# Loading w_in in whole rows, one channel chunk at a time, and holding back one block of x, in a convolution and two-layer MLP kernel

## Chip, cores, metric

One core of one Trainium2 chip. The metric is device microseconds (us) of an execution, lower is better. Most numbers below come from traces: an execution's span, counted from its first instruction, is about 1.7 us shorter than the time measured for it.

## The reference

```python
# x: (8, 4096, 192), weight: (8 heads, 7 taps), w_in: (192, 2048), w_out: (2048, 192)
w = softmax(weight, axis=-1)
y[b, s, h, g] = sum_k w[h, k] * x_pad[b, s + k, h, g]      # causal, 7 taps, 24 channels a head
h = y.reshape(32768, 192) @ w_in
out = maximum(0.01 * h, h) @ w_out                          # float32
```

## The kernel before

The listing is shortened; `...` marks the larger cuts. Two batch rows share the 128 partitions, 64 channels each; 192 channels are three chunks. So w_in is loaded twice, once for each half of the partitions, with a cast from float32 to bf16. The first two blocks of 512 positions go through the machine in halves of 256 ("half 0" to "half 3" of x). VectorE makes most of the convolution, TensorE the two matmuls, ScalarE evicts the first one with the leaky ReLU.

```python
    def load_first(q, after=None):            # x, half q, on the SyncE queue; two stage buffers
        t = stage_pool.tile([128, 2, HS, D], FP32, name="x_nat")
        ...                                   # "after": the load waits for that instruction

    w_in = const_pool.tile([128, NCH, F], BF16)
    for q in range(WQ):                       # WQ = 4 column quarters
        for e in range(2):                    # two halves of the partitions
            fs = slice(q * F // WQ, (q + 1) * F // WQ)
            nc.gpsimd.dma_start(
                out=w_in[e * CH : (e + 1) * CH, :, fs],
                in_=moe_w_in[:, fs].rearrange("(c p) f -> p c f", p=CH),
            )
    w_out = const_pool.tile([128, NFC, D], BF16)
    nc.gpsimd.dma_start(out=w_out, in_=moe_w_out.rearrange("(c p) d -> p c d", p=128))
    ...
    def mm1(grp, u):                          # one unit: 256 columns of h for 256 positions
        ph = psum_h.tile([128, 2, ST], FP32, name="ph", tag="ph")      # two buffers
        for i in range(nf):
            f = nf * u + i
            for c in range(NCH):              # all three chunks close one accumulation
                for e in range(2):
                    nc.tensor.matmul(out=ph[:, e, ...], lhsT=w_in[ps, c, f * 128 : (f + 1) * 128],
                                     rhs=y[ps, c, t0 : t0 + T], start=(c == 0), stop=(c == NCH - 1))
        act = nc.scalar.activation(out=g[blk][...], in_=ph..., func=Prelu, alpha=0.01)
    ...
    for i, grp in enumerate(groups):          # group 0 = half 0, group 1 = half 1, ...
        for j in range(steps):
            for u in range(2 * j, 2 * j + 2):
                mm1(grp, u)
                if i == 0 and u == 3:         # convolution of group 1, chunk 0, on TensorE
                    for job in pe_ahead:
                        job()
            ...                               # second matmul of the group before
            if i == 0 and j == 3:             # cast, transpose and copy half 2
                ...
                transpose_first(2)
                evac_first(2, nc.vector.tensor_copy, nc.vector.tensor_copy)
            for job in ahead[per * j : per * (j + 1)]:
                job()                         # VectorE: convolution of the next group
```

Of the kernel before, what the change touches and what calls it, by code (L numbers as in the profile page):

```python
# [14 lines left out]
def kernel(  # L15
# [8 lines left out]
    nc = tc.nc  # L24

    B, S, D = x.shape
    H, K = weight.shape
    Din, F = moe_w_in.shape
# [6 lines left out]
    CH = 64  # L35
    NCH = D // CH
# [5 lines left out]
    NB = S // ST  # L42
    NBLK = (B // 2) * NB
    LAG = NFC + NFC // 2
    WQ = 4
    NHALF = 5
    NPEC = 2

# [58 lines left out]
    def load_first(q, after=None):  # L107
        t = stage_pool.tile([128, 2, HS, D], FP32, name="x_nat")
        for e in range(2):
            ins = nc.sync.dma_start(  # L110
                out=t[:, e, :, :],
                in_=x[e, q * HT : (q + 1) * HT, :].rearrange("(c p) d -> p c d", p=128),
            )
            if after is not None and e == 0:
                tc.add_manual_dep(
                    ins.ins, after.ins.name,
                    mybir.DependencyInfo(
                        mybir.DependencyClass.Sync, mybir.DependencyReason.DATA
                    ),
                    reason="leave the DMA engines to w_in",  # L120
                )
        x_nat[q] = t

    def cast_first(q, e, copy):
        if q % 2 == 0 and e == 0:
            x_bf[q // 2] = xb_pool.tile([128, NCH, SUB, 2, CH], BF16, name="x_bf")
        h = q % 2
        copy(  # L128
            out=x_bf[q // 2][:, :, h * HS : (h + 1) * HS, e, :],
            in_=x_nat[q][:, e, :, :].rearrange("p s (c k) -> p c s k", c=NCH),  # L130
        )
# [20 lines left out]
    def evac_first(q, *copies):  # L152
        dst = xt[0][:, :, HALO + q * HT : HALO + (q + 1) * HT].rearrange(
            "p c (s i k) -> p i s c k", s=HS, i=2
        )
        for i, t in enumerate(ptr.pop(q)):
            copies[i](out=dst[:, i], in_=t)  # L157
# [4 lines left out]
    def conv_jobs(grp, chunks=range(NCH)):  # L162
        blk, t0, T = grp
        rp, st = divmod(blk, NB)
        if blk not in yt:
            yt[blk] = yt_pool.tile([128, NCH, ST], BF16, name="yt")
        y = yt[blk]
        jobs = []
        for c in chunks:
            for k in range(K):  # L170
                a = BASE + k + st * ST + t0
                src = xt[rp][:, c, a : a + T]
                dst = y[:, c, t0 : t0 + T]
                if k == 0:
                    jobs.append(
                        lambda s=src, d=dst, c=c: nc.vector.tensor_scalar_mul(  # L176
                            d, s, wk[:, c, 0:1]
                        )
                    )
                else:  # L180
                    jobs.append(
                        lambda s=src, d=dst, c=c, k=k: nc.vector.scalar_tensor_tensor(  # L182
                            out=d, in0=s, scalar=wk[:, c, k : k + 1], in1=d,
                            op0=mybir.AluOpType.mult, op1=mybir.AluOpType.add,
                        )
                    )
        return jobs
# [39 lines left out]
    for sign, off in ((1, 0), (-1, GRP - 1)):  # L227
        nc.gpsimd.affine_select(  # L228
            out=sel, in_=sel, compare_op=mybir.AluOpType.is_ge, fill=0.0,
            base=off, channel_multiplier=-sign * GRP,  # L230
            pattern=[[sign * CH, NCH], [0, 2], [sign, CH]],
        )

    w_in = const_pool.tile([128, NCH, F], BF16)
    for q in range(WQ):
        for e in range(2):
            fs = slice(q * F // WQ, (q + 1) * F // WQ)
            nc.gpsimd.dma_start(  # L238
                out=w_in[e * CH : (e + 1) * CH, :, fs],
                in_=moe_w_in[:, fs].rearrange("(c p) f -> p c f", p=CH),  # L240
            )
    w_out = const_pool.tile([128, NFC, D], BF16)
    nc.gpsimd.dma_start(out=w_out, in_=moe_w_out.rearrange("(c p) d -> p c d", p=128))
# [4 lines left out]
    def warm(n):  # L248
# [9 lines left out]
        out=nmax, in_=w9[:, 0:K], axis=mybir.AxisListType.X,  # L258
# [3 lines left out]
        out=w9[:, 0:K], in_=w9[:, 0:K], func=mybir.ActivationFunctionType.Exp,  # L262
# [33 lines left out]
    def diag_high(c):  # L296
        nc.vector.tensor_mul(
            diag[c][:, 0],
            ident2[:, None, :].to_broadcast([128, K, CH]),
            whm[:, c, 0, 0:K, None].to_broadcast([128, K, CH]),  # L300
        )

    def diag_low(c, ks):
        for k in ks:
            act = nc.scalar.activation(  # L305
                out=diag[c][:, 1, k, :], in_=ident2,
                func=mybir.ActivationFunctionType.Copy, scale=whm[:, c, 1, k : k + 1],
            )
        return act

    diag_high(0)
    cast_first(0, 0, nc.vector.tensor_copy)
# [10 lines left out]
    wk = const_pool.tile([128, NCH, K], FP32, name="wk")  # L323
    nc.vector.tensor_mul(wk, wraw[:, :, 0:K], rsum.to_broadcast([128, NCH, K]))
    evac_first(0, nc.vector.tensor_copy, nc.scalar.copy)
    low = diag_low(0, range(2, K))
    diag_high(1)
    diag_low(1, range(K))

# [2 lines left out]
            out=out, in_=in_, func=mybir.ActivationFunctionType.Copy, scale=scale  # L332
        )

    load_first(2, low)
    for n, job in enumerate(conv_jobs(groups[0], range(NPEC, NCH))):
        if n in (4, 5):
            cast_first(1, n - 4, nc.vector.tensor_copy)
        job()
    load_first(3)  # L340
    for c in range(NPEC):
        pe_jobs, evac_y = pe_conv_jobs(groups[0], c)
        for job in pe_jobs:
# [17 lines left out]
    def mm1(grp, u):  # L361
        blk, t0, T = grp
        y = yt[blk]
        nf = ST // T
        ph = psum_h.tile([128, 2, ST], FP32, name="ph", tag="ph")
        for i in range(nf):
            f = nf * u + i
            for c in range(NCH):
                for e in range(2):
                    ps = slice(e * CH, (e + 1) * CH)  # L370
                    nc.tensor.matmul(  # L371
                        out=ph[:, e, i * T : (i + 1) * T],
                        lhsT=w_in[ps, c, f * 128 : (f + 1) * 128],
                        rhs=y[ps, c, t0 : t0 + T],
                        start=(c == 0),
                        stop=(c == NCH - 1),
                    )
        act = nc.scalar.activation(  # L378
            out=g[blk][:, nf * u : nf * (u + 1), :, t0 : t0 + T],
            in_=ph.rearrange("p e (i t) -> p i e t", i=nf),  # L380
            func=mybir.ActivationFunctionType.Prelu, alpha=0.01,
        )
        while unsealed:
            seal[unsealed.pop()] = act.ins.name

    def mm2_one(rt, m, fc):
        b, e, s = subs[m]
# [23 lines left out]
    def mm2_slot(q):  # L411


        n, fc = divmod(q, NFC)
        if n < LAST:
            mm2_one(0, n, fc)
        t1 = q - LAG
        if t1 >= 0:
            mm2_one(1, *divmod(t1, NFC))
            if t1 % NFC == NFC - 1:  # L420
                evac_o(t1 // NFC)
# [18 lines left out]
    for i, grp in enumerate(groups):  # L440
        blk, t0, T = grp
        steps = T // 64
        if t0 == 0:
            g[blk] = g_pool.tile([128, NFC, 2, ST], BF16, name="g", tag="g")
        quota = (avail - slot) // steps

        if i == 0:
            ahead = []
        else:
            ahead = conv_jobs(groups[i + 1]) if i + 1 < len(groups) else []  # L450
        per = -(-len(ahead) // (steps - 1)) if T == ST else -(-len(ahead) // steps)
        for j in range(steps):
            for u in range(2 * j, 2 * j + 2):
                mm1(grp, u)
                if i == 0 and u == 0:
                    pe_ahead, evac_y = pe_conv_jobs(groups[1], 0)
                    ahead = conv_jobs(groups[1], range(1, NCH))
                    per = len(ahead)
                if i == 0 and u == 3:
                    for job in pe_ahead:  # L460
                        job()
                if i == 1 and u in (0, 2):
                    cast_first(3, u // 2, nc.scalar.copy)
            for _ in range(quota):
                mm2_slot(slot)
                slot += 1
            if i == 0 and j == 3:
                evac_y(nc.vector.tensor_scalar_mul)
                for e in range(2):
                    cast_first(2, e, nc.vector.tensor_copy)  # L470
                transpose_first(2)
                evac_first(2, nc.vector.tensor_copy, nc.vector.tensor_copy)
            if i == 1 and j == 1:

                nc.gpsimd.tensor_copy(out=pjunk, in_=g[0][0:1, NFC - 1, 1, HT - 1 : HT])  # L475
                load_x(2)
            if i == 2 and j == 1:
                transpose_x(2)
            for job in ahead[per * j : per * (j + 1)]:
                job()  # L480
            if i == 1 and j == 1:
                transpose_first(3)
                evac_first(3, nc.vector.tensor_copy, nc.vector.tensor_copy)

            last_half = t0 + T == ST
            if j == steps // 4 and last_half:
                load_x(blk + 3)
            if j == steps // 2 and last_half and blk > 0:
                transpose_x(blk + 2)
        avail += 2 * T // 128 * NFC  # L490
# [37 lines left out]
```

## Time and profile before

| | before |
|---|---|
| time, three runs | 698.39 us (698.24 to 699.26) |
| span of the trace | 698.3 us |
| TensorE busy | 689.0 us, 99% |
| first eviction starts | 12.03 us |
| w_in, last load lands | 18.98 us |
| w_out lands | 24.47 us |

TensorE is full from about 25 us to the end, so what a change of the first loads can move is when this full stretch begins. Lines that the prediction shows are not repeated. ScalarE's timeline (start, length, engine, instruction, idle time before it and what ended it):

```profile
12.03 1.94 ACT L378 ACTIVATE g<-ph 128x1024 bf16<-128x1024 f32 x2 [0.81 <-PE ph L371]
14.21 1.94 ACT L378 ACTIVATE g<-ph 128x1024 bf16<-128x1024 f32 x2 [0.24 <-PE ph L371]
17.31 1.94 ACT L378 ACTIVATE g<-ph 128x1024 bf16<-128x1024 f32 x2 [1.17 <-PE ph L371]
19.89 2.97 ACT L378 ACTIVATE g<-ph 128x1024 bf16<-128x1024 f32 x3 [0.64 <-PE ph L371]
```

Eight units of group 0 are evicted from 12.03 to 21.83 with idle gaps of about 2 us.

### The profile page before, as it was taken

What the parts mean: (1) busy time and instruction counts of PE and PEld (TensorE: products, weight loads), DVE (VectorE), ACT (ScalarE), POOL (GpSimd) and SP (SyncE); (2) the same over time, 40 slices, a digit from 0 to 9 for tenths busy, and PEclk for the clock granted to TensorE, in tenths of its full rate; (3) what the DMA queues carried; (4) which work ended last, traced back from release to release, by engine and by line L of the source; (5) the groups of instructions that cost most, each with busy time, mean ns of one, the idle gap of its engine ahead of it and who ended that gap; (6) DMA issues with size and microseconds to landing.
All of it is one profiled execution on the core that took longest, in us unless ns stands there. A gap on an engine that the chain in (4) does not pass through costs nothing.

```text
span 698.3 us, 26019 instructions
## 1 busy us (share of the span) xinstructions
PE 689.0 (99%) x11762; PEld 608.0 (87%) x11762; DVE 542.1 (78%) x1005; ACT 512.1 (73%) x576; POOL 142.3 (20%) x199
## 2 busy tenths in 40 slices
PE   8899999999999999999999999999999999999997
PEld 6799999678888888888888888888888888888887
DVE  7799999967777787777787777787777787777712
ACT  6688888977777777777777777777777777777770
POOL 4722220410222210222211222220222211000000
PEclk9999999999999999999999999999999999999999
DMA  9969554845555535555645556544566625122112
GB/s 170 115 83 104 83 71 81 86 71 76 77 74 83 89 67 76 77 74 84 86 67 79 69 81 81 88 73 71 77 75 81 92 63 77 54 52 58 47 36 69
DMA packets 184847, 54.39 MB, mean 78 GB/s; under 512 B 148384, under 2 KB 184736, under 8 KB 184736
## 3 DMA queue, kind: packets, MB, share of 16 engines
q0 software_dynamic: 98768, 14.17, 29.5%
q1 hardware_dynamic: 85968, 38.56, 23.2%
q8 instruction: 92, 1.51, 0.9%
q14 instruction: 19, 0.16, 0.1%
HBM read 29.88 MB, written 25.17 MB: 79 GB/s over the span
## 4 chain that ended last, share of the span: by engine, by line
PE 94%; DMA 3%; DVE 2%; POOL 0%; issue 0%; ACT 0%; POOLq 0%; ACTq 0%
PE po L391 48%; PE ph L371 46%; DMA w_out<-in_moe_w_out_dram 2%; DVE yt L182 2%; DMA w_in<-in_moe_w_in_dram 1%; POOL sel L228 0%; DVE yt L176 0%; ACT g L378 0%; POOL sel L226 0%; DVE o_sb L430 0%; POOL ident masks.py:199 0%; POOL ident masks.py:197 0%; PE ptr L143 0%; POOLq masks.py:199 0%; ACTq L430 0%
## 5 line engine op out<-in xcount | busy, mean ns | idle before, releaser
L378 ACT ACTIVATE g<-ph 128x1024 bf16<-128x1024 f32 x512 | 496.4, 1021 | 165.7 <-PE ph L371 165.7
L182 DVE SCALAR_TENSOR_TENSOR yt<-xt,wk,yt 128x512 bf16<-128x512 bf16 (+1 forms) x648 | 442.4, 683 | 17.6
L391 PE MATMUL po<-w_out,g 64*128 64x192 bf16 (+1 forms) x8048 | 398.4, 243 | 1.8 <-DMA w_out<-in_moe_w_out_dram 1.8
L391 PEld LDWEIGHTS <-g 64*128 64x128 bf16 (+1 forms) x8048 | 372.3, 94 | 31.1 <-issue 2.2
L371 PE MATMUL ph<-yt,w_in 64*128 64x512 bf16 (+1 forms) x3552 | 393.6, 348 | 2.2 <-ACT g L378 1.2
L371 PEld LDWEIGHTS <-w_in 64*128 64x128 bf16 x3552 | 247.8, 94 | 50.4 <-issue 3.9
L79 POOL DMA_DIRECT2D x_bf<-in_x_dram x180 | 133.7, 774 | 422.4 <-DMA xt<-x_bf 422.4
L430 DVE COPY o_sb<-po 128x192 f32<-128x192 f32 x216 | 77.2, 357 | 127.4 <-PE po L391 125.0
L176 DVE TENSOR_SCALAR yt<-xt,wk 128x512 bf16<-128x512 bf16 (+1 forms) x108 | 36.3, 336 | 0.1
L430 ACT COPY o_sb<-po 128x192 f32<-128x192 f32 x40 | 13.1, 327 | 0.0
L250 PE MATMUL warm<-zero 128*128 128x256 bf16 x24 | 5.2, 371 | 1.1 <-DVE junk L218 1.1
L157 DVE COPY xt<-ptr 128x384 bf16<-128x384 bf16 x7 | 2.2, 351 | 4.4 <-PE ptr L143 4.4
L201 PE MATMUL acc<-xt,diag 64*64 64x256 bf16 x84 | 5.2, 270 | 0.1
L238 POOL DMA_DIRECT2D w_in<-in_moe_w_in_dram x8 | 5.1, 643 | 0.0
L201 PEld LDWEIGHTS <-diag 64*64 64x64 bf16 x84 | 4.3, 106 | 0.8 <-DVE xt L157 0.4
L305 ACT ACTIVATE diag<-ident,whm 128x64 bf16<-128x64 bf16 x14 | 3.6, 335 | 1.9 <-DVE whm L291 1.9
L250 PEld LDWEIGHTS <-zero 128*128 128x128 bf16 x24 | 2.6, 125 | 2.1 <-DVE junk L218 1.1
L475 POOL COPY pjunk<-g 1x1 bf16<-1x1 bf16 x1 | 0.3, 312 | 10.9 <-ACT g L378 10.9
L143 PEld LDWEIGHTS <-x_bf 64*128 64x128 bf16 x48 | 1.4, 94 | 1.0 <-ACT x_bf L128 0.8
L143 PE MATMUL ptr<-ident,x_bf 64*128 64x64 bf16 x48 | 1.7, 191 | 0.5 <-DVE wraw L318 0.5
L128 DVE CAST x_bf<-x_nat 128x384 bf16<-128x384 f32 x5 | 2.2, 449 | 0.0
L255 ACT ACT_TABLE_LOAD x1 | 1.3, 1283 | 0.8 <-PEq L512 0.8
(34 smaller groups left out, 12.2 us busy)
## 6 DMA issues: line engine op xcount, KB each, us to landing
out_dram<-o_sb SPq DMA_DIRECT2D x128, 192.0 KB, 2.2
x_bf<-in_x_dram POOLq DMA_DIRECT2D x180, 64.0 KB, 3.1
x_nat<-in_x_dram SPq DMA_DIRECT2D x8, 192.0 KB, 5.6
w_in<-in_moe_w_in_dram POOLq DMA_DIRECT2D x8, 192.0 KB, 8.7
xt<-x_bf SPq DMA_TRANSPOSE x90, 2.4
w_out<-in_moe_w_out_dram POOLq DMA_DIRECT2D x1, 768.0 KB, 14.7
w<-in_weight_dram SPq DMA_DIRECT2D x1, 0.2 KB
```

The lines of the kernel that those rows point to most:

```text
L79: nc.gpsimd.dma_start(out=t[:, c, :, e, :], in_=src[2 * rp + e, :, :, c * CH : (c + 1) * CH],)
L143: nc.tensor.transpose(out=ts[i][:, s, c, :], in_=x_bf[q // 2][ps, c, (q % 2) * HS + s, :, :].rearrange("p e k -> p (e k)"), identity=ident ...
L176: lambda s=src, d=dst, c=c: nc.vector.tensor_scalar_mul(d, s, wk[:, c, 0:1])
L182: lambda s=src, d=dst, c=c, k=k: nc.vector.scalar_tensor_tensor(out=d, in0=s, scalar=wk[:, c, k : k + 1], in1=d, op0=mybir.AluOpType.mult, ...
L201: lambda k=k, p=p, a=a, e=e, ps=ps: nc.tensor.matmul(out=acc[ps, :T], lhsT=diag[c][ps, p, k, :], rhs=xt[0][ps, c, a : a + T], start=(k == ...
L238: nc.gpsimd.dma_start(out=w_in[e * CH : (e + 1) * CH, :, fs], in_=moe_w_in[:, fs].rearrange("(c p) f -> p c f", p=CH),)
L250: nc.tensor.matmul(out=wa[:, 0, 0:HT], lhsT=zero[:, 0:128], rhs=zero, start=True, stop=True)
L305: act = nc.scalar.activation(out=diag[c][:, 1, k, :], in_=ident2, func=mybir.ActivationFunctionType.Copy, scale=whm[:, c, 1, k : k + 1],)
L371: nc.tensor.matmul(out=ph[:, e, i * T : (i + 1) * T], lhsT=w_in[ps, c, f * 128 : (f + 1) * 128], rhs=y[ps, c, t0 : t0 + T], start=(c == 0) ...
L378: act = nc.scalar.activation(out=g[blk][:, nf * u : nf * (u + 1), :, t0 : t0 + T], in_=ph.rearrange("p e (i t) -> p i e t", i=nf), func=my ...
L391: ins = nc.tensor.matmul(out=po[m], lhsT=g[b][ps, fc, e, s * 128 : (s + 1) * 128], rhs=w_out[ps, fc, :], start=(rt != 1 and fc == 0), stop ...
L430: copy(out=o_sb[:, n % 2, :], in_=po.pop(n))
```

## The change

The intent: long contiguous rows instead of short pieces of columns, and fewer transfers beside the weights. w_in comes in six loads of whole rows (one chunk, one half of the partitions each). x's half 2 is no longer held until ScalarE has made the first diagonals; half 3 is held until the third eviction.

```diff
-    for q in range(WQ):
+    for c in range(NCH):
         for e in range(2):
-            fs = slice(q * F // WQ, (q + 1) * F // WQ)
             nc.gpsimd.dma_start(
-                out=w_in[e * CH : (e + 1) * CH, :, fs],
-                in_=moe_w_in[:, fs].rearrange("(c p) f -> p c f", p=CH),
+                out=w_in[e * CH : (e + 1) * CH, c, :], in_=moe_w_in[c * CH : (c + 1) * CH, :]
             )
...
-    load_first(2, low)
+    load_first(2)
...
-    load_first(3)
...
-                mm1(grp, u)
+                act = mm1(grp, u)
...
+                if i == 0 and u == 2:
+                    load_first(3, act)
```

More of the change, by code (lines that the diff above doesn't have):

```diff
@@ L44 @@
     LAG = NFC + NFC // 2
-    WQ = 4
     NHALF = 5
@@ L119, in load_first @@
                     ),
-                    reason="leave the DMA engines to w_in",
+                    reason="leave the DMA engines to the weights",
                 )
@@ L304, in diag_low @@
         for k in ks:
-            act = nc.scalar.activation(
+            nc.scalar.activation(
                 out=diag[c][:, 1, k, :], in_=ident2,
@@ L308, in diag_low @@
             )
-        return act
     diag_high(0)
@@ L325 @@
     evac_first(0, nc.vector.tensor_copy, nc.scalar.copy)
-    low = diag_low(0, range(2, K))
+    diag_low(0, range(2, K))
     diag_high(1)
@@ L384, in mm1 @@
             seal[unsealed.pop()] = act.ins.name
+        return act
     def mm2_one(rt, m, fc):
```

## The prediction

> **What bounds the kernel now.** I read the page first, then the chain of work that ended last, the waits, the transfers and clock of the first 30 us in windows, and the timelines of VectorE and TensorE up to 125 us. From the page:
>
> ```profile
> PE 689.0 (99%) x11762; PEld 608.0 (87%) x11762; DVE 542.1 (78%) x1005; ACT 512.1 (73%) x576; POOL 142.3 (20%) x199
> PE 94%; DMA 3%; DVE 2%; POOL 0%; issue 0%; ACT 0%; POOLq 0%; ACTq 0%
> ```
>
> TensorE is busy for 689.0 of 698.3 us. The change touches only the loads of the first 25 us, so all that it can move is the start; the 3% that the chain gives to DMA is this stretch of the chain:
>
> ```profile
> 2.90 6.58 DMA w_in<-in_moe_w_in_dram
> 9.48 0.28 issue
> 9.77 14.70 DMA w_out<-in_moe_w_out_dram
> 24.47 0.04 issue
> 24.51 1.33 PE po L391 x14
> ```
>
> The ninth GpSimd load (w_out, after eight of w_in) is issued only at 9.77, when the first w_in load has landed, and lands at 24.47; only then can the second matmul (po) start. The longest waits of the first 40 us that involve weights are small:
>
> ```profile
> PEld L371 <- DMA w_in<-in_moe_w_in_dram: 2.2, 2, 1.3
> PE po L391 <- DMA w_out<-in_moe_w_out_dram: 1.8, 1, 1.8
> POOL w_out L243 <- DMA w_in<-in_moe_w_in_dram: 1.8, 1, 1.8
> ```
>
> Windows on the clock show that the wait for w_out costs more than its 1.8 us (columns: stretch, then length and busy time of PE, PEld, DVE, ACT, POOL, then clock, DMA share, GB/s):
>
> ```profile
> 22.26:25.67 3.41, 1.61 (x25) 1.41 (x22) 3.23 (x7) 1.92 (x3) 3.41 (x5) 1.00 0.95 68
> 25.67:29.08 3.41, 3.41 (x32) 2.56 (x31) 1.48 (x4) 1.59 (x3) 3.41 (x6) 0.50 1.37 87
> ```
>
> After a window in which PE was busy for 1.61 us, it runs 3.41 us at half clock: 1.7 us lost.
>
> Last, a bound that the shares hide. VectorE's and TensorE's timelines:
>
> ```profile
> 20.70 0.62 DVE L157 COPY xt<-ptr 128x384 bf16<-128x384 bf16 x2 [1.14 <-PE ptr L143]
> 30.49 0.62 DVE L157 COPY xt<-ptr 128x384 bf16<-128x384 bf16 x2 [3.23 <-PE ptr L143]
> 120.59 1.04 PE L371 MATMUL ph<-yt,w_in 64*128 64x512 bf16 x8 [0.25 <-DVE yt L182]
> ```
>
> From 30.49 to past 120 us VectorE has no idle gap at all (convolutions back to back); at 120.59 TensorE waits 0.25 us for it. Up to 120 us the two are level: a delay of VectorE's start at 20.70 beyond its 3.23 us of later idle, or of TensorE's, reaches the end.
>
> **What the Trainium skill says.** (1) "DMA: Bandwidth & Descriptors", section "Issuing engines are not separate DMA queues": loads from different engines share the same 16 DMA engines and interleave. The trace agrees: from 13 to 16 us, queue 0 (weights) and queue 1 (x) both move, and w_in slows against 9 to 11 us, when it is alone. In the order 6 to 8, 9 to 11, 13 to 16 (two lines) and 20 to 21 us (packets, MB as written, share):
>
> ```profile
> q0 software_dynamic: 194, 0.19, 79.0%
> q0 software_dynamic: 406, 0.38, 120.9%
> q0 software_dynamic: 412, 0.39, 77.3%
> q1 hardware_dynamic: 403, 0.29, 39.6%
> q0 software_dynamic: 498, 0.19, 158.6%
> ```
>
> (2) The same page, "Rules for kernel authors", says to coalesce small transfers and that transfers to disjoint partition halves serialize. Here the gain of larger pieces looks small: w_in with 1 KB written per packet goes at 0.19 MB/us, and w_out with 384 B per packet also at 0.19 MB/us (498 packets). Written bytes are bf16 and read bytes float32, so both read about 0.38 MB/us; packet size doesn't show. (3) "SBUF — State Buffer", section "SBUF: two separate sides", describes that GpSimd can be kept from writing descriptors while VectorE holds the shared port. That could explain the slow 6 to 8 us (0.10 MB/us with VectorE busy 2.83 of the 3 us from 5 to 8), but the trace before doesn't prove it. (4) "TensorE: Matmul & The Clock Gate", Part 1, says that about 3.4 us of idleness halves the clock; the trace agrees, 3.41 us at 0.50 above, though PE wasn't wholly idle there.
>
> **The change part by part.**
>
> *Order of w_in.* Before, four column quarters x two halves: the first two loads (landed 9.48 and 10.41 by the transfer records) suffice for a quarter of the first matmul's work, so it starts at 10.79, and the last quarter lands at 18.98. After, a chunk of channels at a time: every output needs all three chunks, so the first accumulation can't close before all six loads have landed. Call that time T.
>
> *T.* The first w_in packet starts at 4.80 (packet records; issue at 2.90). 8 x 192 KB = 1.57 MB at 0.19 MB/us: 8.2 us. Into the same time fall the rest of halves 0 and 1 of x (158 packets of 768 B after 5 us, 0.12 MB, 0.3 us at 0.38 MB/us) and most of half 2 (0.39 MB, 0.9 us): half 2 is now issued near 6 us, when its stage buffer is free (casts end at 5.76), not at 8.0. Half 3 and w_out, which before mixed with w_in from 12 to 18.5 us, no longer do. Engines don't finish together (before, w_out packets appear at 16.2 while w_in's last starts at 18.54); I allow 0.9 us. T = 4.8 + 8.2 + 0.3 + 0.9 + 0.9 = 15.1. If the slow start of 5 to 9 us persists, which cost about 1.7 us of full rate, T is 16.8; if long rows run somewhat faster, 14.
>
> *From T to the second matmul.* Eight units of the first matmul (12 matmuls of 64x256, 0.74 us) are each evicted by ScalarE (1.94 us for two, 0.97 each) out of two PSUM buffers; between units 4 and 5 stand 28 convolution matmuls (1.72 us). Stepping this through: unit 0 needs 8 more matmuls, 0.5 us; evictions end at T+1.55, 2.45, 3.45, 4.4; the convolution runs until T+5.1; evictions 5 to 8 end at T+6.95, 7.85, 8.85, 9.8; transposes of half 2 end at T+9.15, and VectorE's copies of them begin at T+9.2; two more units, and the second matmul begins at T+10.7. With T = 15.1: copies at 24.3, second matmul at 25.8. TensorE idles from about 11 to 15, so the half clock probably comes here (12 matmuls then take 1.4 us, more than an eviction): about 0.75 us more on this path.
>
> *What it gives back.* w_out is the seventh load, not the ninth, so it needn't wait for a landing; its packets follow w_in on each engine, 4.1 us (0.79 MB at 0.19), landing by about 21: before it is needed at 25.8. The wait of 1.8 us goes, and with it the half-clock window, 1.7 us.
>
> *Half 3 held.* Issued after the third eviction (about 18.5), with some 4 us to land; cast at T+11 = 26. Hidden. The cast of half 1 may be delayed by long w_in packets in turn with it, to 10 or 12; VectorE has room until T.
>
> *Sum.* TensorE: before, 24.51 + 1.7 = 26.2 at full-clock reckoning; after, 25.8 without and 26.5 with a cold window: -0.4 to +0.3 us. VectorE: before, copies at 20.70 + 3.23 us idle = 23.9 as the effective start of the unbroken run; after, 24.3 to 25.0, with no idle left: +0.4 to +1.1 us, and this one is the later. About +0.7 us: 698.4 + 0.7 = 699.1.
>
> **Rivals.** (a) Whole rows load much faster, T near 13: everything shifts by -2 us, and no cold window comes: about 696.5. For it: the slow 5 to 9 us, and a quarter as many descriptors; against: equal read rates at 768 and 2048 B. (b) The slow start stays and the cold window doubles, T near 17: about 701.5. For it: TensorE would be idle for nearly two windows. (c) x's half 1 is starved, as one 768 B packet waits for an 8 KB one: VectorE's convolution of the second group moves right. It matters only if half 1 lands after about 14 us (it landed at 8.31), then +1 us or more. (d) All is hidden, since w_out is no longer late: 698.4.
>
> **Range and chances.** T between 13 and 17 gives 696.8 to 701.5. 2% is 14 us, more than the whole prologue that the weights bound (24.5 us, most of it needed anyway) could plausibly give or take: same is nearly sure.
>
> **What would show it.** Right: six w_in loads, landing together by 15; no wait for w_out; the first eviction near 15.7 against 12.03; half-clock window around 15 to 19 instead of 25.67; VectorE's copies near 24.5, no 3.23 us gap after. Wrong: T below 13.5 or above 17, w_out still waited for, or VectorE idle between 25 and 120 us.

## The result, and the profile after

The kernel after took 702.26 us (median of 4 runs, 701.76 to 703.34), the kernel before 698.83 (4 runs). The ratio is 1.0049 (95% interval 1.003 to 1.0068). Here and below a ratio is the mean time of one kernel's runs over that of the other's of the same rounds, so not quite the ratio of the medians quoted. Executions over 1.5% slower than the fastest of the same kernel are left out of the means. 702.26 lies outside the range of 696.8 to 701.5. In class it is "same", as forecast: slower by half a per cent.

The chain of the kernel after (start, length, what; pieces of 0.2 us and less left out). L367 is the first matmul, L374 its eviction, L156 the copies of x's transposes, L181 the convolution:

```profile
5.60 11.25 DMA w_in<-in_moe_w_in_dram
16.90 0.62 PE ph L367 x7
17.54 1.03 ACT g L374
18.61 2.66 PE ph L367 x24
21.28 1.65 PE acc L200 x28
22.93 0.78 PE ph L367 x12
23.73 1.95 ACT g L374 x2
25.72 0.83 PE ph L367 x12
26.76 0.62 DVE xt L156 x2
```

The sixth load of w_in lands at 16.85, 2.1 us earlier than the eighth before. But the first eviction starts at 17.54 instead of 12.03, because no accumulation could close earlier. From there the chain runs as stepped through in the prediction, and the copies of half 2 start at 26.75 instead of 20.70. w_out landed at 21.48 and nobody waited for it.

The clock, in windows (stretch, length, busy time of PE, PEld, DVE, ACT, POOL, then granted clock, DMA share, GB/s):

```profile
14.24:17.65 3.41, 1.03 (x15) 0.78 (x17) 3.20 (x8) 0.11 (x1) 0.00 (x0) 1.00 1.41 209
17.65:21.07 3.42, 3.33 (x33) 2.15 (x29) 2.64 (x6) 2.89 (x3) 0.00 (x0) 0.50 0.84 101
```

TensorE idled while it waited for w_in and then ran one window at half clock, as forecast. VectorE's and TensorE's timelines of the kernel after:

```profile
26.75 0.62 DVE L156 COPY xt<-ptr 128x384 bf16<-128x384 bf16 x2 [2.63 <-PE ptr L142]
33.01 0.61 DVE L156 COPY xt<-ptr 128x384 bf16<-128x384 bf16 x2
48.40 0.29 DVE L175 TENSOR_SCALAR yt<-xt,wk 128x256 bf16<-128x256 bf16 x1 [0.39 <-DMA xt<-x_bf]
123.90 0.82 PE L367 MATMUL ph<-yt,w_in 64*128 64x512 bf16 x6 [1.40 <-DVE yt L181]
```

The 3.23 us gap of before is gone, VectorE runs through but for 0.39 us, and TensorE waits for it at 123.90, where before the same unit resumed at 120.59. It is the first of 512 positions, called the wide unit below. After it both traces have 577.7 us left (701.6 - 123.90 and 698.3 - 120.59). So the whole difference arises before it, and I use the time of the wide unit below as a clean measure of a trace.

### The profile page after: what moved, and what is told of

The parts are those of the page before. It is cut to its first block, busy times and chain, and to the rows that moved or that the text cites. A ratio compares the mean times of both kernels' runs of the same rounds, so it can differ in the third digit from the quotient of the medians.

```text
span 701.6 us, 26018 instructions
## 1 busy us (share of the span) xinstructions
PE 691.1 (99%) x11762; PEld 610.3 (87%) x11762; DVE 542.3 (77%) x1005; ACT 512.5 (73%) x576; POOL 140.3 (20%) x197
## 4 chain that ended last, share of the span: by engine, by line
PE 83%; DVE 11%; DMA 3%; POOL 1%; issue 1%; ACT 1%; POOLq 0%; ACTq 0%
PE po L388 42%; PE ph L367 41%; DVE yt L181 10%; DMA w_in<-in_moe_w_in_dram 2%; DVE yt L175 1%; POOL x_bf L78 1%; DMA xt<-x_bf 1%; ACT g L374 1%; DMA x_bf<-in_x_dram 1%; POOL w_in L237 0%; PE acc L200 0%; DVE xt L156 0%; POOL sel L227 0%; POOL sel L225 0%; DVE o_sb L427 0%
## 5 line engine op out<-in xcount | busy, mean ns | idle before, releaser
L374 ACT ACTIVATE g<-ph 128x1024 bf16<-128x1024 f32 x512 | 496.6, 1021 | 166.8 <-PE ph L367 166.8
L181 DVE SCALAR_TENSOR_TENSOR yt<-xt,wk,yt 128x512 bf16<-128x512 bf16 (+1 forms) x648 | 442.4, 683 | 17.6
L367 PE MATMUL ph<-yt,w_in 64*128 64x512 bf16 (+1 forms) x3552 | 393.9, 348 | 5.5 <-DVE yt L181 2.4
L367 PEld LDWEIGHTS <-w_in 64*128 64x128 bf16 x3552 | 249.0, 94 | 52.9 <-issue 5.8
L474 POOL COPY pjunk<-g 1x1 bf16<-1x1 bf16 x1 | 0.2, 176 | 20.3 <-ACT g L374 20.3
L156 DVE COPY xt<-ptr 128x384 bf16<-128x384 bf16 x7 | 2.2, 350 | 2.6 <-PE ptr L142 2.6
L237 POOL DMA_DIRECT2D w_in<-in_moe_w_in_dram x6 | 3.3, 580 | 0.0
```

Source lines behind the costliest of these rows:

```text
L156: copies[i](out=dst[:, i], in_=t)
L181: lambda s=src, d=dst, c=c, k=k: nc.vector.scalar_tensor_tensor(out=d, in0=s, scalar=wk[:, c, k : k + 1], in1=d, op0=mybir.AluOpType.mult, ...
L237: nc.gpsimd.dma_start(out=w_in[e * CH : (e + 1) * CH, c, :], in_=moe_w_in[c * CH : (c + 1) * CH, :])
L367: nc.tensor.matmul(out=ph[:, e, i * T : (i + 1) * T], lhsT=w_in[ps, c, f * 128 : (f + 1) * 128], rhs=y[ps, c, t0 : t0 + T], start=(c == 0) ...
L374: act = nc.scalar.activation(out=g[blk][:, nf * u : nf * (u + 1), :, t0 : t0 + T], in_=ph.rearrange("p e (i t) -> p i e t", i=nf), func=my ...
```

## The experiments

All ran on one core, in four groups, each on another chip; kernels of a group shared the runs of the kernel before. The labels in brackets name the runs below. The spread of before was wide (697.44 to 704.37 over 11 runs in the first group), so small ratios are read together with the traces. The mean granted clock that the record lists for each run explains most of it. Of the 33 timed runs of before in three groups, 23 have 0.999 or 1.000 and took 697.18 to 699.47 us; nine have 0.994 to 0.997 and took 700.20 to 704.37 (five, two and two in a group); one lies between. One half-clock window of 3.41 us takes about 0.0024 off the mean of such a run, so the 23 had no full window and the nine had at least one. All ten timed runs of after have 0.994 to 0.998. Where it says "sorted by clock" below, runs were split in this way after the fact.

**Rows alone** (p1). Before, with the loads of w_in from after; x as before.

```diff
-    for q in range(WQ): ... column quarters
+    for c in range(NCH): ... whole rows
```

> The kernel before with w_in alone changed (six loads of whole rows, chunk by chunk); x halves 2 and 3 as before. Theory A (the order costs: every first accumulation waits for the last of six loads, and the slowest DMA engine sets it): the last w_in load lands at 16.9 to 17.6 us, the first eviction starts at 17.6 to 18.3, no wait for w_out, about +3.5 us against before (ratio 1.004 to 1.007). Rival B (the loss comes from moving x: half 2 early and half 3 late): within 1 us of before.

702.03 us against 699.31; ratio 1.0028 (0.9999 to 1.0057). The last load landed at 15.89, earlier than expected, the first eviction started at 17.00, the copies of half 2 at 25.66. The delay of the start is there with this part alone; the ratio is on the slow side but its interval just touches 1. All six runs have a clock of 0.997 or less, so none is without a half-clock window, against five of the eleven of before beside them.

**x alone** (p2). After, with the old quarters.

```diff
-    for c in range(NCH): ... whole rows
+    for q in range(WQ): ... column quarters
```

> The kernel after with the old column quarters (eight loads) in place of rows; half 2 early and half 3 held stay. Theory A: the x part is no loss but a gain, since half 3 leaves the DMA engines to the weights: last quarter lands near 18 instead of 18.98, w_out near 22.7 instead of 24.47, the half-clock window goes, VectorE's 3.23 us gap shrinks; 1 to 3 us faster than before (ratio 0.996 to 0.9985). Rival B: 2 to 4 us slower than before (1.003 to 1.006).

699.48 against 699.31, ratio 0.9993 (0.9961 to 1.0024). First eviction at 12.03, copies at 20.65. Neither theory's number came: no loss, and no gain to be seen. The interval excludes the loss of rival B (1.003 to 1.006) but not all of the gain of theory A. Sorted by clock it is the same: the three runs without a half-clock window took 697.97 to 698.40, the five of before 697.44 to 698.98. w_out landed at 24.95 and was waited for by 2.59 us. The two moves of x together aren't where the loss comes from.

**Half 2 held** (h2, repeated as h2b). After, with half 2 of x held until the first eviction.

```diff
-    load_first(2)
...
+                if i == 0 and u == 0:
+                    load_first(2, act)
```

> The kernel after with half 2 of x held until the first eviction, so that only halves 0 and 1 share the DMA engines with w_in. If half 2's packets stretch w_in as I reckoned (0.9 us), the last w_in load lands near 16.0 instead of 16.85 and the time falls by 0.5 to 0.9 us against after (near 701.4). If the late engines are late for another reason (lag got before 8 us), it stays at 16.5 to 16.9 and the time within 0.3 us of after.

701.79, ratio 1.0024 (0.9992 to 1.0055). The last load landed at 14.90. This trace has no half-clock window, and its copies start at 23.88, 8.98 us after the landing; with the window that distance is 9.76 to 9.98 in the seven other traces of this order that have just one. The run was the fastest of its six, so I repeated it:

> The kernel with half 2 of x held until the first eviction, once more. If half 2's packets are what moved the last w_in load from 14.90 to 16.85, it lands at 14.7 to 15.5 again, and the time is 1 to 2 us below that of after on the same chip. If the 14.90 was scatter, it lands above 16.

15.60 this time, just past the 15.5 expected, copies at 25.36, with the window; 701.63 against 698.42, ratio 1.0046 (1.0031 to 1.0062), 0.96 us below a2 in the medians. With half 2 beside it w_in landed at 15.69 to 16.88 in the five traces that start as after does (after, a2, a3, wm, dv), without it at 14.90 and 15.60. So half 2 costs about 1 us of landing time on average, near the 0.9 reckoned, though the two groups nearly touch; and even without it the landing is later than the 14.2 that the prediction's sum leaves.

**Short pieces, same order** (sp). After, with the tile of w_in padded so that each row lands in four pieces of 1 KB.

```diff
-    w_in = const_pool.tile([128, NCH, F], BF16)
+    w_in = const_pool.tile([128, NCH, 4, F // 4 + 32], BF16)
...
-                out=w_in[e * CH : (e + 1) * CH, c, :], in_=moe_w_in[c * CH : (c + 1) * CH, :]
+                out=w_in[e * CH : (e + 1) * CH, c, :, 0 : F // 4],
+                in_=moe_w_in[c * CH : (c + 1) * CH, :].rearrange("p (q f) -> p q f", q=4),
```

> The kernel after with the same six loads in the same order, but w_in's tile padded so that each row lands as four pieces of 1 KB (1536 packets, not 384). If packet length is without effect on the rate, the bulk is the same, and x's half 1, no longer taking turns with 4 KB packets, lands near 8.3 instead of 11.8; last w_in load at 16 to 17, time within 0.7 us of after. If long rows load faster (the intent of the change), the last load is over 1 us later than 16.85 and the time over 1 us above after. If long packets cause the lag of the slow engines, the last load lands 1 us or more earlier and the time falls by 1 us or more.

703.27, ratio 1.005 (1.0018 to 1.0082). The last load landed at 16.33, half 1 of x at 8.24 instead of 11.81. The latter says little: with pieces of 4 KB half 1 landed at 8.35 in p1 and at 8.65 in h2b. Half 2 says more: it landed at 15.37, against 17.10 to 17.98 in the five traces that start as after does. So with short pieces x waits less in its turn with w_in, but the length doesn't decide when w_in is there. The queue lines from 6 to 8 us (packets, MB, share of 16 engines) of after, of short pieces in rows and of quarters (x alone), in that order:

```profile
q0 software_dynamic: 92, 0.32, 88.7%
q0 software_dynamic: 365, 0.36, 108.8%
q0 software_dynamic: 193, 0.18, 82.0%
```

In all nine traces of rows the weights' queue moved 0.29 to 0.36 MB in these 2 us, in six of quarters 0.18 to 0.22, with pieces of 4 KB or of 1 KB in the rows alike; two column halves (below) moved 0.29. The rows do load faster at the start, and not because their packets are long. Whether the order in the source, the number of loads or their shape does it, these runs don't separate.

**Two column halves** (q2). After, with two column halves (WQ = 2, four loads) in place of rows.

```diff
-    for c in range(NCH): ... whole rows
+    for q in range(2): ... column halves
```

> The kernel after with w_in in two column halves (four loads, 2 KB written per packet), the rest as after. Theory A (after loses because the first accumulation waits for all of w_in): the first two loads land near 10.5, the first eviction starts near 12.0 as before, the last load lands near 15.5 and is not waited for, w_out lands near 21 and is not waited for, no half-clock window near 25; VectorE's copies of half 2 start near 20.3 and its 3.23 us gap is gone. 3 us or more faster than before (near 695.5, ratio 0.993 to 0.997). Rival (rows and order do not matter, the loss is elsewhere): within 1 us of after.

697.94 against 698.03, ratio 0.9992 (0.9971 to 1.0013). The first half landed at 12.53, not 10.5, so the first eviction started at 13.44, not 12.0, and the copies at 21.94, not 20.3; the last load landed at 18.02 and w_out at 23.57, not 21. VectorE has no gap after the copies and w_out isn't waited for, as expected. So the loss goes when an early part of the columns is complete early, as the order theory says; the gain over before that I expected isn't there. The expected 0.993 to 0.997 was wrong.

**A filler for the clock** (wm). After, with 24 idle matmuls before the first unit.

```diff
     transpose_first(1)
+    warm(24)
```

> The kernel after with 24 idle matmuls between the transposes of half 1 and the first matmul, to keep TensorE's clock up while it waits. If the half-clock window is a cost of its own, no 0.50 window between 15 and 22 us in the trace, copies of half 2 start 9.2 us after the last w_in load instead of 9.9, and the time falls by 0.7 us against after. If the wait for w_in hides it, no change.

701.84, ratio 1.005 (1.0026 to 1.0073). The half-clock window came all the same, at 17.88: the filler was over before TensorE's longest waits. Its last w_in load, at 16.88, repeats that of after. The trace doesn't answer the question, but the list of runs does in part. Sorted by clock, three of the six runs are without a half-clock window (0.999 and 1.000) and took 701.08 to 701.42; the three with one took 702.26 to 704.21; the nine of before in this group without one took 697.18 to 699.47, 698.06 on average. So the window is a cost of its own, between 1 and 3 us, but about 3.2 us of the loss are there without it: that the window alone makes the loss is ruled out, as far as three runs can.

**VectorE relieved** (dv). After, without the last four convolution steps of the fourth group (wrong result).

```diff
+            if i == 2:
+                ahead = ahead[:-4]
```

> The kernel after with the last four convolution steps of the fourth group left out on VectorE (wrong result on purpose; 1.9 us of VectorE work). If VectorE's unbroken run carries the delay, TensorE's wait for yt near 124 us (1.4 us) goes and the time falls by 1.2 to 1.5 us against after. If TensorE alone sets the end, no change.

701.93, ratio 1.0046 (1.0025 to 1.0067): no gain, TensorE still waits 1.00 us near 123. The trace says why (VectorE's timeline, the first convolution of block 2):

```profile
47.71 0.29 DVE L175 TENSOR_SCALAR yt<-xt,wk 128x256 bf16<-128x256 bf16 x1 [2.17 <-DMA xt<-x_bf]
```

The time taken away became a wait for the transposed x of block 2. Two things end just before these transposes. They are issued behind an output store on SyncE's queue (store at 42.98, transposes from 43.47), and the store follows TensorE. And they need block 2's loads on GpSimd's queue, issued from 27.41 on, after ScalarE's last eviction of group 0, the last of which landed at 43.56. In after SyncE waited 1.2 us for that landing. So the theory that VectorE alone carries the delay falls: VectorE and these two paths, all of which start from the late evictions, are level near 48 us.

**VectorE burdened** (da). Before, with four more steps in the fourth group (wrong result).

```diff
+            if i == 2:
+                ahead = ahead + ahead[:4]
```

> The kernel before with four more convolution steps on VectorE in the fourth group (wrong result on purpose; 1.8 us of VectorE work). If VectorE and TensorE are level up to 120 us, TensorE's wait near 121 us grows from 0.25 to about 2 us and the time rises by 1.5 to 1.9 us against before. If TensorE alone sets the end, no change.

699.97 against 698.03; ratio 1.002 (0.9997 to 1.0042), so about 1.4 us, with an interval that includes none. But two of the eleven runs of before had a half-clock window and none of the six here; sorted by clock it is 700.01 against 698.06 on average, 1.9 us. TensorE's wait near 121 us didn't grow to 2 us, as expected; its timeline shows where the time goes:

```profile
45.40 0.83 PE L371 MATMUL ph<-yt,w_in 64*128 64x256 bf16 x12 [1.55 <-DVE yt L182]
120.20 1.04 PE L371 MATMUL ph<-yt,w_in 64*128 64x512 bf16 x8 [0.52 <-DVE yt L182]
```

TensorE waits 1.55 us for VectorE one group later, a wait that no trace of before has. More work on VectorE before 120 us isn't free; less of it brings nothing.

**After once more** (a2).

> The kernel after once more, on the chip of the next three. Its last w_in load landed at 16.85 us; the two runs since with the same start had 16.88 and 16.59. Expected 16.5 to 17.0 again, and 3 to 4 us slower than before (ratio 1.004 to 1.006). If it lands below 16.0, the landing scatters from run to run and half 2 can't be blamed from one trace.

702.59 against 698.42; ratio 1.0059 (1.0045 to 1.0073). The last load landed at 16.56, copies at 26.32, the wide unit at 123.31. As expected.

**A mixed order, and the same with half 2 held** (mx, mh). The first quarter in columns, the rest in rows; group 1's convolution on TensorE moved to the wait.

```diff
+    for e in range(2): ... columns 0 to 511, three chunks in one load
     for c in range(NCH):
-        for e in range(2): ... whole rows
+        for e in range(2): ... columns 512 to 2047
...
-                if i == 0 and u == 3:
+                if i == 0 and u == 1:
                     for job in pe_ahead:
```

> The kernel after with the first column quarter of w_in loaded first (two loads, as in before) and the other three quarters in rows, chunk by chunk (six loads); the convolution of the second half-block moved from after unit 3 to after unit 1. Theory A: the first eviction starts near 12 us as in before, the last load lands at 16 to 17, six units remain after it, copies of half 2 start about 5.6 us later (near 22), w_out is not waited for: 1 to 2.5 us faster than before (ratio 0.9965 to 0.9985). Rival (whatever is loaded in rows costs): slower than before by 1 us or more.

700.59 against 698.42; ratio 1.0027 (1.0012 to 1.0041). The first eviction came at 12.26 and the last load at 16.99, as expected, but the copies at 23.54, not 22 (half-clock window from 17.23), and that is no gain, since before has them at 20.88 to 22.17 in its usual runs (below).

> The mixed order with half 2 of x held until the first eviction (near 13 us), half 3 until the third. Theory: last w_in load at 15 to 16, copies of half 2 near 21, 2 to 3.5 us faster than before (ratio 0.995 to 0.997). If half 2 now comes too late (lands after 20 us), VectorE waits for it and it is no better than the mixed order without the hold.

698.87 against 698.42; ratio 1.0005 (0.9991 to 1.0019). Last load at 16.59, copies at 22.43, half 2 waited for by 0.86 us. It gives back what rows lost, and no more. No version that I ran beats before.

**Before, profiled three more times** (b2, b3, b4), because the anchor of the sum was in doubt; single runs, whose state is unknown, so only their traces are used.

> The kernel before, profiled again. The one trace of before (its own time 699.96 us, while its median is near 698.4) waits 1.8 us for w_out and then has a half-clock window at 25.67. If that trace is typical: w_out waited for and the window there again, span near 698.3. If it fell in a bad phase of the clock's windows: no half-clock window near 25 us, span near 696.7.

> As b2_before: typical would be a window at half clock near 25 us and a span near 698.3; otherwise no window there and a span near 696.7.

> As b2_before: typical would be a window at half clock near 25 us and a span near 698.3; otherwise no window there and a span near 696.7.

Spans 697.0, 696.8, 697.3. None has a half-clock window near 25 us, though each waits for w_out, 1.25, 0.20 and 1.13 us. b2, in the windows of its clock, where the first trace had 1.61 us busy and then 0.50:

```profile
21.98:25.40 3.42, 2.09 (x30) 1.89 (x31) 3.21 (x8) 2.38 (x4) 3.33 (x6) 1.00 0.74 55
25.40:28.80 3.40, 3.40 (x74) 3.23 (x71) 2.28 (x6) 2.35 (x3) 3.40 (x5) 1.00 1.37 87
```

And VectorE's later gap, with TensorE's wait for it, in b2:

```profile
28.46 0.62 DVE L157 COPY xt<-ptr 128x384 bf16<-128x384 bf16 x2 [1.02 <-PE ptr L143]
119.38 1.04 PE L371 MATMUL ph<-yt,w_in 64*128 64x512 bf16 x8 [1.06 <-DVE yt L182]
```

**After, a third time** (a3).

> The kernel after, profiled a third time: last w_in load at 16.5 to 16.9 us, half-clock window starting at 16 to 18 us, span 700 to 702.

Span 701.0. The last load landed at 15.69, earlier than expected and under the 16.0 that a2's expectation set as the mark of scatter, but two windows in a row were at half clock (14.73 to 21.56) and the copies began at 26.56.

The traces side by side (us; "idle" is VectorE's later gaps between the copies and the wide unit):

| | last w_in | copies of half 2 | idle | wide unit | span |
|---|---|---|---|---|---|
| before | 18.98 | 20.70 | 3.23 | 120.59 | 698.3 |
| b2 | 19.16 | 20.88 | 1.02 | 119.38 | 697.0 |
| b3 | 18.68 | 21.96 | 0.24 | 119.16 | 696.8 |
| b4 | 20.27 | 22.17 | 0.92 | 119.67 | 697.3 |
| after | 16.85 | 26.75 | 0.39 | 123.90 | 701.6 |
| a2 | 16.56 | 26.32 | none | 123.31 | 701.0 |
| a3 | 15.69 | 26.56 | 0.17 | 123.38 | 701.0 |

## Why the prediction was wrong, point by point

**Right: the mechanism.** The order delays the first eviction to T, and the step from T to the copies held: predicted T + 9.2, or about 9.95 with a half-clock window; measured 9.9 in after (26.75 - 16.85), 9.76 in a2, 8.98 in h2 without the window. That VectorE's gap is used up and that TensorE then waits for it was right too. That VectorE's path "is the later" isn't shown: taking 1.9 us of work from it brought nothing (dv).

**Wrong: the size of T.** The step that failed is "I allow 0.9 us" for engines that don't finish together. The sum before it came out right: 4.8 + 8.2 + 0.3 + 0.9 = 14.2, and in the packet records of after the first packet of w_out starts at 13.92, so by then one DMA engine was done with w_in. That was partly luck: by 8 us w_in had moved 0.39 MB, where 0.19 MB/us from 4.80 on gives 0.61, and from 5 to 14 us x had moved 0.28 MB, where 0.12 + 0.39 were reckoned; the two errors offset each other. From 13.92 to the landing took 2.9 us (16.85), 2.6 in a2, and 1.7 and 2.25 without half 2. The trace of before had it: 16.22 to 18.98 is 2.8 us, and the prediction quotes both times. T was 16.4 on average of after, a2 and a3, 1.3 us over 15.1.

The trace holds sixteen completion marks for each load. Of the sixth load's, fifteen had come by 15.96 in after and by 15.58 in a2, and the last came 0.9 and 1.0 us later; in a3 all had come by 15.69. So one late part makes the difference between a T near 15.7 and one near 16.7. Why it lags isn't settled: the records used here don't tell the engines apart. Rival (b) named 16.8 for a slow start that stays. The start got faster than before (0.39 against 0.25 MB by 8 us), though not full, so (b) was right in part; what the sum lacked was the tail.

**Wrong: what the change "gives back".** "The wait of 1.8 us goes, and with it the half-clock window, 1.7 us" treated one trace as the kernel. That execution had taken 699.96 us, its kernel's median is 698.4, and I added the difference to the median. In three more traces the window is absent, and so it is in 23 of the 33 timed runs (above). The wide unit of before is at 119.4 on average of b2, b3 and b4, not 120.59: 1.2 us of the predicted credit didn't exist in a usual run.

**The sum again.** Predicted +0.7. The copies started at 26.54 on average of the three traces of after, against 24.65, the middle of 24.3 to 25.0: +1.9, of which 1.3 is T and the rest that the half-clock window came in each of them, in one twice. The anchor: +1.2. Together 3.8; the wide units of the three traces of each kernel differ by 4.1 (123.5 - 119.4), and 0.3 stays unexplained but for the 0.39 of one trace. The medians differ by 3.4 and 4.2 us in the two jobs that timed after.

**Small steps.** That w_out needn't wait for a landing was true and worth nothing: in both kernels w_out's first packets start before w_in has landed (16.22 against 18.98, 13.92 against 16.85), so the issue at 9.77 came in time. Half 3 was hidden, as said. Half 1 was delayed (11.81 against 8.31), as rival (c) feared, and VectorE waited 2.04 us for it, within the room that it had until T. The shared port that the prediction names under (3) doesn't explain the slow start: from 5 to 8 us VectorE was busy for 2.83 us in before, x alone, after and short pieces alike, while w_in had moved 0.25, 0.26, 0.39 and 0.41 MB by 8 us.

**Where the rows' gain went.** w_in as a whole lands 2 us earlier than before. It isn't used: before takes up its first quarter at 12 to 14 us (first eviction at 12.03, 12.05, 13.67 and 13.88 in its four traces) and gets the others in step with ScalarE, so the landing of the last quarter at 19 is nearly hidden, whereas after needs everything at once at the start.

## What to carry to other kernels

The time at which a large load is complete is worth nothing by itself; ask when each consumer can close its first accumulation, and order the loads so that each one completes some outputs. When a wait ends with the last of several loads, take the time from the first engine that is done to the landing from the trace; here it was 1.7 to 3.0 us in nine traces of rows and 2.8 to 4.7 in six of quarters. Before working out a change of under one per cent from one trace, compare that run's own time, and its granted clock, with those of the kernel's other runs.

## What the Trainium skill lacked or had wrong

- "DMA: Bandwidth & Descriptors", section "Rules for kernel authors", advises to coalesce many small transfers, those under 64 KB above all. The loads here are of 192 KB and more, so no run tests this. That page has no measured delay for a load that takes turns with longer pieces of another: half 2 of x landed at 17.10 to 17.98 us in five traces beside 4 KB pieces, and at 15.37 in one beside 1 KB pieces.
- The same page's section "Latency and other measured facts" says that DMA engines 7 and 15 are usually slower; it gives no size. Here the time from the first engine that was done to the landing was 1.7 to 4.7 us. Which engines were late, no run here shows.
- No page that I read says how pieces of columns compare with whole rows of one matrix: from 6 to 8 us quarters moved 0.18 to 0.22 MB, two column halves 0.29, rows 0.29 to 0.36.
- "TensorE: Matmul & The Clock Gate", Part 1, speaks of idle and busy windows without saying how busy is enough. In the eighteen traces here, up to 40 us, each window at full clock in which TensorE was busy for 1.79 us or less of 3.41 was followed by one at half clock (11 cases, 0.51 to 1.79), and none with 1.90 or more was. In a3 a window at half clock with 2.80 us busy was followed by a second one; one with 2.96 in sp was not.
